# First batch of a fused attention and expert kernel: another order of filler, scores, values and sums of x, and k of batch two on one engine

## The chip, the cores and the metric

The kernel runs on one core of a Trainium2 chip. The core has five engines, each with a queue of its own that runs in order: TensorE (PE in the profile, with its weight loads as PEld), VectorE (DVE), ScalarE (ACT), GpSimd (POOL) and SyncE (SP), which here only issues DMAs. They wait for each other on semaphores. The metric is the device time of one execution in microseconds (us).

## The reference

```python
def _attn_ref(q, k, v):                      # 8 batches, 8 heads, 576 rows, 64 columns
    k_p = k.reshape(B, H, Sp, pool, D).mean(axis=3)     # pool = 8, Sp = 72
    v_p = v.reshape(B, H, Sp, pool, D).mean(axis=3)
    scores = scale * np.matmul(q, k_p.transpose(0, 1, 3, 2))
    scores = scores - np.max(scores, axis=-1, keepdims=True)
    attn = np.exp(scores)
    attn = attn / (np.sum(attn, axis=-1, keepdims=True) + 1e-09)
    return np.matmul(attn, v_p)
def _moe_ref(x, w_in, w_out, alpha):         # x: 4608 x 512, w_in: 512 x 2048
    h = x @ w_in
    s = np.sin(alpha * h)
    g = h + s * s / (alpha + 1e-09)
    return g @ w_out
```

x is the output of the attention, with the heads side by side. All is float32.

## The kernel before, in words

**Hidden layer.** `hidden` computes h = x w_in and g for nine tiles u of 512 rows of x. Rows and columns are halved twice, and seven block products take the place of eight: p1 to p7, in the order 1, 5, 6, 2, 7, 3, 4. Their left sides are sums of blocks of w_in, made by `combine_w_in` (L638; four steps: s1 = a21 + a22, s2 = s1 - a11, a21 = a11 - a21, s4 = a12 - s2), their right sides sums of blocks of x, made by `sums_of_x` (L740; four steps, of which step 1 needs step 0 and step 3 needs step 1). The columns of w_in come in four parts J. So a tile u has 28 slots, seven for each J. In each slot TensorE runs one product (L767, four instructions of 128x256, eight records in the profile), and the queue of work `left` does what the product of the slot before made possible: copies and sines on ScalarE, additions on VectorE (L746, L838).

**Attention beside it.** The attention of batch u + 1 is written by hand into the slots of tile u: `carry(u)` puts functions into a table by slot, and `hidden` calls those of a slot ahead of its product. Each engine's queue has the order in which the functions are called, so an instruction that waits holds all that stand behind it on its engine. Scores of a batch (L288) need k, summed over eight rows by GpSimd (`pool_rows`, L120, three additions) and turned by TensorE (`k_t`, L250). exp is on ScalarE, the sum and its reciprocal on VectorE and the multiplication on GpSimd (`norm`, L345). `turn` (L469 to L479) transposes 32x32 blocks on VectorE, and `move` (L489) brings them into the tile aM with 16 DMAs in two parts on SP's queue. `all_values` (L565, L578) multiplies aM with the sums of v in slot 25 or 26 and gives x of the next tile. k of a batch is loaded in two halves (`load_k`, L108) into one of two buffers, `kvin`, that v uses too.

**The first batch** has no tile ahead of it to hide behind. `first_batch` handles its heads in four pairs. k's rows are added (`load_k_heads`, L162 and L164, on VectorE for pairs one and two, on GpSimd for three and four); `k_head` and `k_last` (L354, L360) turn and sum them on TensorE, `q_head` (L371) turns q, `products_head` (L392) makes the scores, `soft_shift` (L398, L400) subtracts the largest, `soft_exp` (L406) takes exp, `norm_head` (L412, L413, L418) sums and divides. `a_head` (L446 to L453) turns the weights of two pairs. `sum_v_rest` and `sum_v_rows` (L181, L191) sum v on TensorE. `values` (L535, L537) multiplies weights and v for two pairs into two PSUM banks, and `to_x` (L504, or L506 on VectorE) copies them to x. `fill` (L878) puts in products of a tile of ones, `full`, whose result is not used; `first_batch` makes it (L872). Pairs three and four are finished in slots 1 and 2 of tile 0, where also one half of k of batch two is summed by VectorE (`half_k`, L113); the other half is GpSimd's.

Where it matters below: L600 turns alpha, L601 to L610 make its reciprocal, L150 and L152 add k's last rows, L945 is one more unused product that keeps an order, L93 copies q of batch two, L262 and L251 copy turned q and k, L807 and L809 are copies of `left`, and L954 clears a part of aM.

Of the kernel before, what the change touches and what calls it, by code (L numbers as in the profile page):

```python
# [13 lines left out]
F32 = mybir.dt.float32  # L14
AX = mybir.AxisListType.X
AF = mybir.ActivationFunctionType
OP = mybir.AluOpType
PSUM = bass.MemoryType.PSUM

P = 128  # L20
POOL = 8
TH = 256
# [18 lines left out]
class Kernel:  # L41
# [58 lines left out]
        return (qm[:, 0:n].rearrange("p (h t d) -> p h t d", h=self.H, t=4),  # L100
                qm[:64, n:].rearrange("p (h d) -> p h d", h=self.H))

    def load_k(self, b, e, later=False):

        Sp, D, NP = self.Sp, self.D, self.NP
        m = Sp // 3
        t = self.kvp.tile([P, 2048], F32, name="kvin")[:NP * m, 0:3 * POOL * D]
        self.nc.sync.dma_start(out=t, in_=self.k[b, NP * e:NP * e + NP].rearrange("h (p x) d -> (h p) (x d)", x=3 * POOL))  # L108
        if b not in self.kp:
            self.kp[b] = self.ap.tile([NP * m, 3, 2, D], F32, name="kp")  # L110
        t, out = t.rearrange("p (j x) -> p j x", j=3), self.kp[b][:, :, e, :]
        if later:
            return lambda: self.nc.vector.tensor_reduce(out=out, in_=t.rearrange("p j (t d) -> p j d t", t=POOL), axis=AX, op=OP.add)  # L113
        self.pool_rows(t, out)

    def pool_rows(self, t, out):
# [113 lines left out]
    def attention(self, b):  # L230

        nc, D, H, Sp, NP, S = self.nc, self.D, self.H, self.Sp, self.NP, self.S
# [255 lines left out]
                        r, w = 64 * s + 32 * c, 704 if c else 736  # L488
                        nc.sync.dma_start(out=self.aM[r:r + 32, a, 0:w], in_=tr[32 * a:32 * a + 32, c, s, 0:w])  # L489

        def to_x(ps, hp, t0, m, s0=0, eng=nc.scalar):

            while s0 < m:
                u, x0 = divmod(b * S + t0 + s0, 2 * TH)
                w = min(m - s0, 2 * TH - x0)
                if u not in self.xT:
                    self.xT[u] = self.home(u % 3, [P, self.K1, 2 * TH])
                x = self.xT[u][:, hp, x0:x0 + w]
                if t0:
                    y = ps[..., s0:s0 + w]  # L500
                else:
                    x, y = x.rearrange("p (j t) -> p j t", t=4), ps[:, s0 // 4:(s0 + w) // 4, :]
                if eng is nc.scalar:
                    nc.scalar.mul(out=x, in_=y, mul=1.0 / POOL)  # L504
                else:
                    nc.vector.tensor_scalar(out=x, in0=y, scalar1=1.0 / POOL, scalar2=None, op0=OP.mult)  # L506
                s0 += w

        def value_parts(hp, rest):
# [16 lines left out]
            return ([(vm[64 * s:64 * s + 64, 2 * g + e], at(64 * s, 64, 2 * g + e)) for e in range(2)],  # L526
                    (vz[r:r + 32, 2 * g:2 * g + 2], at(r, 32, 4)))

        def values(hps, banks, engines, n=1):

            ps = [self.psum([P, 4 * P], i) for i in banks]
            parts = [value_parts(hp, False) for hp in hps]
            for o, (main, _) in zip(ps, parts):
                for e, (w, x) in enumerate(main):
                    nc.tensor.matmul(o[64 * e:64 * e + 64], w, x, start=True, stop=False, skip_group_check=True)  # L535
            for o, (_, (w, x)) in zip(ps, parts):
                nc.tensor.matmul(o, w.rearrange("p e d -> p (e d)"), x, start=False, stop=True, skip_group_check=True)  # L537
            for i in range(n):
                for hp, o, eng in zip(hps, ps, engines):
                    to_x(o.rearrange("p (t j) -> p j t", t=4), hp, 0, 512 // n * (i + 1), 512 // n * i, eng)  # L540

        def values_rest(banks):

# [185 lines left out]
        self.aturn = (self.aturn + 1) % 3  # L729
        return self.psum(shape, 5 + self.aturn)  # L730

    def sums_of_x(self, u, n, kk=slice(0, 2)):

        nc = self.nc
        if u not in self.bt:
            self.bt[u] = self.home(3, [P, 4, 2, TH])
        xT, bt = self.xT[u], self.bt[u]
        B = lambda i, j: xT[:, 2 * i:2 * i + 2, j * TH:(j + 1) * TH]
        o, x, y = ((0, B(0, 1), B(0, 0)), (1, B(1, 1), bt[:, 0]), (2, B(1, 1), B(0, 1)), (3, B(1, 0), bt[:, 1]))[n]
        nc.vector.tensor_tensor(out=bt[:, o, kk], in0=x[:, kk], in1=y[:, kk], op=OP.subtract)  # L740

    def hidden(self, u, extra):

# [112 lines left out]
    def first_batch(self):  # L856

        nc = self.nc
        self.att = [self.attention(b) for b in range(self.B)]
        A = self.att[0]  # L860
# [7 lines left out]
        self.load_q_heads(0, 0, 2, nc.scalar)  # L868
        add_k = [self.load_k_heads(0, nc.sync, nc.vector)]
        one = self.sm.tile([P, 1], F32, name="one")  # L870
        full = self.tp.tile([P, P], F32, name="full")
        nc.vector.memset(full[:], 1.0)  # L872
        nc.scalar.activation(out=one[:], in_=self.ident[:, 0:1], func=AF.Sqrt)

        def fill(n):

            for _ in range(n):
                nc.tensor.matmul(self.PS[:, 0, 3 * P:4 * P], full[:], full[:], start=True, stop=True)  # L878
        fill(5)
        self.turn_alpha()  # L880
        refine = self.root()
# [16 lines left out]
        self.load_w_in_part(0)  # L898
        self.q_rest = self.A[3][:64, 0, 512:1024].rearrange("p (h d) -> p h d", h=self.H)
        A.new_a()  # L900
        fill(4)
        A.k_head(0)
        add_rest()
        A.q_head(0)
        A.k_last()
        for f in add_k[1:]:
            f()
        fill(2)
        A.products_head(0)
        A.k_head(1)  # L910
        A.q_head(1)
        A.soft_shift(0)
        A.soft_exp(0)
        refine()
        fill(2)
        A.products_head(1)
        A.k_head(2)
        A.q_head(2)
        A.soft_shift(1)
        A.soft_exp(1)  # L920
        A.norm_head(0, nc.gpsimd)
        fill(2)
        A.products_head(2)
        self.sum_v_rest(0, 0)
        A.k_head(3)
        A.q_head(3)
        A.norm_head(1, nc.vector)
        fill(2)
        A.products_head(3)
        A.soft_shift(2)  # L930
        self.sum_v_rows(0, 0, 2)
        A.a_head(0, (1, 7, 0))
        A.soft_exp(2)
        A.soft_shift(3)
        A.soft_exp(3)
        self.sum_v_rows(0, 1, 2)
        A.norm_head(2, nc.gpsimd)
        A.norm_head(3, nc.vector)
        self.load_q_rest(0, self.q_rest)
        self.load_k(1, 0)  # L940
        self.half_k = self.load_k(1, 1, True)
        self.load_q(1)
        self.load_w_in_part(1)
        A.values((0, 1), (5, 6), (nc.scalar, nc.scalar), 2)
        nc.tensor.matmul(self.psum([P, 4 * P], 4), full[:], far[0][:, 0:4 * P], start=True, stop=True)  # L945
        self.combine_w_in(0, (0,))
        self.sums_of_x(0, 0)
        self.combine_w_in(0, (1,))
        self.combine_w_in(0, (2, 3), nc.gpsimd)

    def carry(self, u):

# [3 lines left out]
        b = u + 1  # L956
        if u == 0:
            A0, A = self.att[:2]
            at(1, A0.rest_q)
            at(1, A0.a_head, 1, (5, 7, 2))  # L960
            at(1, self.half_k)
            at(2, A0.values, (2, 3), (2, 1), (self.nc.vector, self.nc.scalar))
            for kk in range(2):
                at(2, self.sums_of_x, 0, 1, slice(kk, kk + 1))
            at(2, A0.score, 4)
            at(2, self.sums_of_x, 0, 2)
            at(2, self.sums_of_x, 0, 3)
            at(2, self.load_w_in_part, 2)
            at(2, self.load_w_in_part, 3)
            at(2, self.pairs_q, 1, range(5))  # L970
            at(4, self.combine_w_in, 1, (0, 1, 2, 3), self.nc.gpsimd)
            at(4, A.q_t, 0, self.nc.vector.tensor_copy)
            at(4, A.q_t, 1, self.nc.vector.tensor_copy)
            at(4, A.k_t)
            at(7, self.load_v, 1)
            at(7, lambda: self.pool_v())
            for i in range(2):
                at((5, 10)[i], A.two_scores, i)
            at(11, A.two_shifts)
            for i in range(2, 5):  # L980
                at(5 + i, A.q_t, i)
            at(9, A0.exp, 4)
            for i in range(4):
                at((9, 9, 15, 15)[i], A.exp, i)
                at((10, 10, 16, 16)[i], A.norm, i)
                at((13, 13, 17, 18)[i], A.turn, i)
            at(8, self.combine_w_in, 2, (0, 1, 2, 3), self.nc.gpsimd)
            at(13, A0.norm_rest)
            at(14, self.combine_w_in, 3, (0, 1), self.nc.gpsimd)
            at(17, self.combine_w_in, 3, (2, 3), self.nc.gpsimd)  # L990
            at(23, A0.a_rest)
            at(24, lambda: A0.values_rest((5, 6, 7, (self.turn + 1) % 5)))
            for r in (32, 96):
                at(3, self.nc.gpsimd.memset, self.aM[r:r + 32, :, 704:736], 0.0)
            at(18, A.move, 0)
            at(18, A.move, 1)
            at(26, A.all_values)
            at(9, self.load_q, 2)
            at(14, self.load_q, 3)
            for e in range(2):  # L1000
                at(17, self.load_k, 2, e)
            at(27, self.att[2].k_t)
            turn = 23
        else:
            at(0, self.sums_of_x, u, 2)
            at(0, self.sums_of_x, u, 3)
        if 0 < u < last:
# [6 lines left out]
                at((9, 10, 11, 12)[i], A.norm, i)  # L1014
                at((12, 12, 13, 13)[i], A.turn, i)
            at(14, A.move, 0)
            at(14, A.move, 1)
            at(6, self.load_v, b)
            at(12, lambda: self.pool_v())
            for i in range(2):  # L1020
                if b < last:
                    at((12, 17)[i], self.load_k, b + 1, i)
            at(25, A.all_values)
            if b < last:
                at(26, self.att[b + 1].k_t)
# [216 lines left out]
    def run(self):  # L1242
        nc, tc = self.nc, self.tc
        pool = lambda s, n, b, **kw: s.enter_context(tc.tile_pool(name=n, bufs=b, **kw))
        with ExitStack() as top:
            const = self.const = pool(top, "const", 1)
            self.tp = pool(top, "tp", 1)
            self.PS = pool(top, "ps", 1, space=PSUM).tile([P, 8, 512], F32, name="PS")
            self.aturn = 0
            ident = self.ident = const.tile([P, P], F32, name="ident")  # L1250
            make_identity(nc, ident)
            engines = {nc.tensor.engine, nc.vector.engine, nc.scalar.engine, nc.gpsimd.engine, nc.sync.engine}
# [98 lines left out]
```

## Time and profile before

| | |
|---|---|
| median of 7 runs | 926.2 us (923.79 to 926.81) |
| the profiled execution | 926.2 us |
| its span, first to last instruction | 924.4 us |
| mean granted TensorE clock | 0.998 |
| first product of the hidden layer starts | 26.89 us |
| p6 and p3 of the first part start | 38.41 and 48.77 us |

The profile is of one execution. A line of a view names the engine, the line of the kernel, the operation, what is written and read (home are tiles of x and sums of x, a and as blocks of w_in and their sums, PS is PSUM, ex the scores), the shape and how often (x). The waits view puts idle time of an engine down to the instruction that ended it. A float32 matmul leaves two records.

### The profile page before, as it was taken

The numbers are of one execution on the slowest core, as the hardware profiler recorded it, in microseconds if no ns is written. First come the engines' busy times: TensorE is split into PE (matmuls) and PEld (weight loads), VectorE is DVE, ScalarE is ACT, GpSimd is POOL, SyncE is SP. The second block draws the span as 40 slices with busy tenths as digits, with TensorE's granted clock in tenths as the row PEclk, the third lists the DMA queues.
The fourth block names the chain that finished last, engine by engine and source line by source line (L and its number), as shares of the span: only waits on it lengthen the run. The fifth ranks groups of instructions, "written<-read, shape, count | busy, mean of one in ns | idle before, by whom it ended". The sixth has DMA issues, their size and how long they took to land.

```text
span 924.4 us, 17756 instructions
## 1 busy us (share of the span) xinstructions
PE 906.8 (98%) x7025; PEld 820.8 (89%) x7025; DVE 669.4 (72%) x1010; ACT 436.2 (47%) x996; POOL 159.6 (17%) x153
## 2 busy tenths in 40 slices
PE   7899999999999999999999999999999999999997
PEld 6587787888878888788888899999999999999997
DVE  6874764746657475673466989988888888988894
ACT  3577586776857668586886631211111111112111
POOL 2747062160612506141000000000000000000000
PEclk9999999999999999999999999999999999999999
DMA  9846666867568755646527237171626353433401
GB/s 272 224 149 180 173 170 194 225 187 174 154 190 212 202 134 156 199 110 220 197 92 235 87 112 228 30 225 33 192 65 173 85 168 90 149 109 115 143 15 39
DMA packets 134731, 141.13 MB, mean 153 GB/s; under 512 B 49832, under 2 KB 103224, under 8 KB 134648
## 3 DMA queue, kind: packets, MB, share of 16 engines
q1 hardware_dynamic: 133304, 138.54, 52.1%
q10 hardware_dynamic: 1344, 1.45, 0.5%
q8 instruction: 56, 0.92, 0.5%
q14 instruction: 27, 0.22, 0.1%
HBM read 75.37 MB, written 47.19 MB: 133 GB/s over the span
## 4 chain that ended last, share of the span: by engine, by line
PE 79%; DVE 6%; SPq 6%; DMA 3%; POOL 2%; issue 2%; ACT 1%; DVEq 0%; POOLq 0%; ACTq 0%
PE PS L1107 41%; PE PS L767 33%; SPq L489 5%; DMA kvin<-in_k_dram 3%; PE PS L288 2%; POOL kvin L120 2%; DVE tr L469 1%; DVE h L746 1%; DVE sm L343 1%; SPq L845 1%; PE PS L878 1%; PE PS L565 1%; DVE home L740 0%; PE PS L250 0%; POOL kp L120 0%
## 5 line engine op out<-in xcount | busy, mean ns | idle before, releaser
L767 PE MATMUL PS<-home,a 128*128 128x256 f32 x1152 | 264.7, 381 | 1.6 <-DVE h L746 1.4
L767 PEld LDWEIGHTS PS<-home,a 128*128 128x128 f32 x1152 | 217.1, 190 | 38.0 <-issue 4.8
L767 PE MATMUL PS<-home,as 128*128 128x256 f32 x864 | 201.7, 383 | 2.9 <-DVE home L740 2.9
L767 PEld LDWEIGHTS PS<-home,as 128*128 128x128 f32 x864 | 163.4, 191 | 26.9 <-DVE home L740 3.7
L1107 PE MATMUL PS<-s,wb 128*128 128x144 f32 x896 | 119.3, 286 | 0.4 <-ACT PS L1220 0.4
L1107 PEld LDWEIGHTS PS<-s,wb 128*128 128x128 f32 x896 | 113.7, 190 | 0.7 <-ACT PS L1220 0.6
L780 ACT ACTIVATE s<-s,c 128x256 f32<-128x256 f32 (+1 forms) x216 | 110.2, 574 | 0.0
L746 DVE TENSOR_TENSOR h<-PS,p 128x512 f32<-128x512 f32 x72 | 49.1, 684 | 80.6 <-PE PS L767 42.7
L773 ACT ACTIVATE s<-h,al 128x256 f32<-128x256 f32 x144 | 65.2, 505 | 59.4 <-DVE h L746 58.6
L1220 ACT COPY PS<-PS 128x144 f32<-128x144 f32 x56 | 14.7, 263 | 146.0 <-PE PS L1107 141.7
L773 ACT ACTIVATE s<-PS,al 128x256 f32<-128x256 f32 x144 | 60.1, 469 | 32.9 <-PE PS L767 20.9
L1107 PE MATMUL PS<-r,wb 128*128 128x144 f32 x512 | 73.2, 286 | 0.0
L1107 PE MATMUL PS<-s,a 128*128 128x144 f32 x512 | 73.2, 286 | 0.0
L838 DVE TENSOR_TENSOR h<-PS,s 128x512 f32<-128x512 f32 x36 | 24.7, 686 | 65.2 <-ACT s L780 65.2
L120 POOL TENSOR_TENSOR kvin<-kvin 96x768 f32<-96x768 f32 (+3 forms) x40 | 63.1, 1578 | 47.5 <-DMA kvin<-in_k_dram 43.1
L1107 PEld LDWEIGHTS PS<-r,wb 128*128 128x128 f32 x512 | 67.1, 190 | 0.1
L1107 PEld LDWEIGHTS PS<-s,a 128*128 128x128 f32 x512 | 67.0, 190 | 0.0
L345 POOL TENSOR_TENSOR ex<-ex,sm 128x576 f32<-128x576 f32 (+1 forms) x28 | 35.0, 1272 | 183.8 <-ACT PS L807 163.2
L1239 ACT COPY PS<-PS 128x144 f32<-128x144 f32 x56 | 14.7, 263 | 88.4 <-PE PS L1107 88.4
L1107 PE MATMUL PS<-s,we 128*128 128x144 f32 x384 | 54.9, 286 | 0.0
L1107 PE MATMUL PS<-x,wb 128*128 128x144 f32 x384 | 54.9, 286 | 0.0
L1107 PEld LDWEIGHTS PS<-s,we 128*128 128x128 f32 x384 | 50.4, 190 | 0.1
(191 smaller groups left out, 1214.5 us busy)
## 6 DMA issues: line engine op xcount, KB each, us to landing
g_bridge<-h SPq DMA_DIRECT2D x72, 512.0 KB
r<-g_bridge SPq DMA_DIRECT2D x31, 1152.0 KB
out_dram<-o SPq DMA_DIRECT2D x128, 72.0 KB
kvin<-in_k_dram SPq DMA_DIRECT2D x14, 576.0 KB
q<-in_q_dram SPq DMA_DIRECT2D x7, 1024.0 KB
kvin<-in_v_dram SPq DMA_DIRECT2D x14, 512.0 KB
aM<-tr SPq DMA_DIRECT2D x56, 92.0 KB
aM<-tr SPq DMA_DIRECT2D x56, 88.0 KB
```

The source lines that it names most:

```text
L120: self.nc.gpsimd.tensor_tensor(out=t[..., 0:w] if w > D else out, in0=t[..., 0:w], in1=t[..., w:2 * w], op=OP.add)
L288: nc.tensor.matmul(ps[e][r0 + r:r0 + r + q.shape[-1], h, :], q[s], kb[s, hp, :], start=True, stop=True)
L345: nc.gpsimd.tensor_tensor(out=E(i), in0=E(i), in1=sm.unsqueeze(2).to_broadcast([P, n, Sp]), op=OP.mult)
L489: nc.sync.dma_start(out=self.aM[r:r + 32, a, 0:w], in_=tr[32 * a:32 * a + 32, c, s, 0:w])
L746: add = lambda o, x, y: nc.vector.tensor_tensor(out=o, in0=x, in1=y, op=OP.add)
L767: nc.tensor.matmul(ps[:, jj, :], self.A[p][:, kk, f * P:(f + 1) * P], x[:, kk, :], start=(start and jj == 0 and kk == 0), stop=(kk == 1), ...
L773: nc.scalar.activation(out=G.s[:, i, jj, j, :], in_=src[:, jj], func=AF.Sin, scale=self.al[:, f:f + 1])
L780: nc.scalar.activation(out=x, in_=x, func=AF.Square, scale=self.c[:, f:f + 1])
L838: add = lambda o, x, y: self.nc.vector.tensor_tensor(out=o, in0=x, in1=y, op=OP.add)
L1107: nc.tensor.matmul(out, W[:, J // 2, J % 2, :], A[:, J, :], start=(start and J == 0), stop=(J == self.NJ - 1), skip_group_check=True)
L1220: nc.scalar.copy(out=x1[:, 0, :], in_=x0[:, 1, :])
L1239: nc.scalar.copy(out=x1[:, 1, :], in_=x1[:, 0, :])
```

## The change

What is done in the first batch, and the order in which it is issued:

- `full` is a constant now, written by VectorE before the identity is made. The fills are 5, 3, 3, 3, 2 instead of 5, 4, 2, 2, 2, 2.
- products_head(3) comes behind a_head(0) (which turns the weights of pairs one and two). norm_head(1) comes right behind norm_head(0); sum_v_rest behind q_head(3). soft_exp(3) and norm_head(3) come behind the values of the first two pairs. The second sum_v_rows goes to slot 1 of tile 0.
- sums_of_x(0, 0) and (0, 1) are gone. `values` makes the two differences of x itself: the second half of the values in PSUM, times 1/8, minus the first half of x, or minus the difference before, in one VectorE instruction for each pair and half. All copies to x are ScalarE's.
- combine_w_in for J = 0: step s1 goes to GpSimd, the last two steps go from GpSimd to VectorE, in slot 2. s2 stays on VectorE.
- Both halves of k of batch two are summed on GpSimd.

In the slots: turn of the last tile of scores and the 16 moves of batch two go from slot 18 to slot 19 of tile 0. In the tiles after it the second half of k is loaded in slot 14, between the two parts of the moves, instead of in slot 17.

```diff
-    def load_k(self, b, e, later=False):
+    def load_k(self, b, e):
...
-        if later:
-            return lambda: self.nc.vector.tensor_reduce(out=out, in_=t.rearrange("p j (t d) -> p j d t", t=POOL), axis=AX, op=OP.add)
         self.pool_rows(t, out)
...
-        def values(hps, banks, engines, n=1):
+        def values(hps, banks, n, d):
...
+            if d == 0:
+                self.bt[0] = self.home(3, [P, 4, 2, TH])
+            turned = [o.rearrange("p (t j) -> p j t", t=4) for o in ps]
             for i in range(n):
-                for hp, o, eng in zip(hps, ps, engines):
-                    to_x(o.rearrange("p (t j) -> p j t", t=4), hp, 0, 512 // n * (i + 1), 512 // n * i, eng)
+                for hp, o in zip(hps, turned):
+                    to_x(o, hp, 0, 512 // n * (i + 1), 512 // n * i)
+            for kk, o in enumerate(turned):
+                y = self.bt[0][:, 0, kk] if d else self.xT[0][:, kk, 0:TH]
+                f = lambda x: x.rearrange("p (j t) -> p j t", t=4)
+                nc.vector.scalar_tensor_tensor(out=f(self.bt[0][:, d, kk]), in0=o[:, TH // 4:TH // 2, :], scalar=1.0 / POOL, in1=f(y),
+                                               op0=OP.mult, op1=OP.subtract)
...
-        fill(4)
+        fill(3)
         A.k_head(0)
         add_rest()
         A.q_head(0)
         A.k_last()
         for f in add_k[1:]:
             f()
-        fill(2)
+        fill(3)
         A.products_head(0)
...
         refine()
-        fill(2)
+        fill(3)
         A.products_head(1)
...
         A.norm_head(0, nc.gpsimd)
+        A.norm_head(1, nc.vector)
         fill(2)
         A.products_head(2)
-        self.sum_v_rest(0, 0)
         A.k_head(3)
         A.q_head(3)
-        A.norm_head(1, nc.vector)
-        fill(2)
-        A.products_head(3)
+        self.sum_v_rest(0, 0)
         A.soft_shift(2)
         self.sum_v_rows(0, 0, 2)
         A.a_head(0, (1, 7, 0))
+        self.combine_w_in(0, (0,), nc.gpsimd)
+        A.products_head(3)
         A.soft_exp(2)
         A.soft_shift(3)
-        A.soft_exp(3)
-        self.sum_v_rows(0, 1, 2)
         A.norm_head(2, nc.gpsimd)
-        A.norm_head(3, nc.vector)
         self.load_q_rest(0, self.q_rest)
-        self.load_k(1, 0)
-        self.half_k = self.load_k(1, 1, True)
+        for e in range(2):
+            self.load_k(1, e)
         self.load_q(1)
         self.load_w_in_part(1)
-        A.values((0, 1), (5, 6), (nc.scalar, nc.scalar), 2)
-        nc.tensor.matmul(self.psum([P, 4 * P], 4), full[:], far[0][:, 0:4 * P], start=True, stop=True)
-        self.combine_w_in(0, (0,))
-        self.sums_of_x(0, 0)
+        A.values((0, 1), (5, 6), 2, 0)
+        nc.tensor.matmul(self.psum([P, 4 * P], 4), self.full[:], far[0][:, 0:4 * P], start=True, stop=True)
+        A.soft_exp(3)
+        A.norm_head(3, nc.vector)
         self.combine_w_in(0, (1,))
-        self.combine_w_in(0, (2, 3), nc.gpsimd)
...
+            at(1, self.sum_v_rows, 0, 1, 2)
             at(1, A0.rest_q)
             at(1, A0.a_head, 1, (5, 7, 2))
-            at(1, self.half_k)
-            at(2, A0.values, (2, 3), (2, 1), (self.nc.vector, self.nc.scalar))
-            for kk in range(2):
-                at(2, self.sums_of_x, 0, 1, slice(kk, kk + 1))
+            at(2, A0.values, (2, 3), (2, 1), 1, 1)
             at(2, A0.score, 4)
             at(2, self.sums_of_x, 0, 2)
             at(2, self.sums_of_x, 0, 3)
+            at(2, self.combine_w_in, 0, (2, 3))
...
-                at((13, 13, 17, 18)[i], A.turn, i)
+                at((13, 13, 17, 19)[i], A.turn, i)
...
-            at(18, A.move, 0)
-            at(18, A.move, 1)
+            at(19, A.move, 0)
+            at(19, A.move, 1)
...
             at(14, A.move, 0)
-            at(14, A.move, 1)
...
-                    at((12, 17)[i], self.load_k, b + 1, i)
+                    at((12, 14)[i], self.load_k, b + 1, i)
+            at(14, A.move, 1)
...
+            full = self.full = const.tile([P, P], F32, name="full")
+            nc.vector.memset(full[:], 1.0)
             ident = self.ident = const.tile([P, P], F32, name="ident")
```

More of the change, by code (lines that the diff above doesn't have):

```diff
@@ L489, in move, with to_x @@
                         nc.sync.dma_start(out=self.aM[r:r + 32, a, 0:w], in_=tr[32 * a:32 * a + 32, c, s, 0:w])
-        def to_x(ps, hp, t0, m, s0=0, eng=nc.scalar):
+        def to_x(ps, hp, t0, m, s0=0):
             while s0 < m:
@@ L502, in to_x @@
                     x, y = x.rearrange("p (j t) -> p j t", t=4), ps[:, s0 // 4:(s0 + w) // 4, :]
[L503 to L506, printed above, removed]
+                nc.scalar.mul(out=x, in_=y, mul=1.0 / POOL)
                 s0 += w
@@ L730, in abank, with sums_of_x @@
         return self.psum(shape, 5 + self.aturn)
-    def sums_of_x(self, u, n, kk=slice(0, 2)):
+    def sums_of_x(self, u, n):
         nc = self.nc
@@ L739, in sums_of_x @@
         o, x, y = ((0, B(0, 1), B(0, 0)), (1, B(1, 1), bt[:, 0]), (2, B(1, 1), B(0, 1)), (3, B(1, 0), bt[:, 1]))[n]
-        nc.vector.tensor_tensor(out=bt[:, o, kk], in0=x[:, kk], in1=y[:, kk], op=OP.subtract)
+        nc.vector.tensor_tensor(out=bt[:, o], in0=x, in1=y, op=OP.subtract)
     def hidden(self, u, extra):
@@ L870, in first_batch @@
         one = self.sm.tile([P, 1], F32, name="one")
-        full = self.tp.tile([P, P], F32, name="full")
-        nc.vector.memset(full[:], 1.0)
         nc.scalar.activation(out=one[:], in_=self.ident[:, 0:1], func=AF.Sqrt)
@@ L877, in fill @@
             for _ in range(n):
-                nc.tensor.matmul(self.PS[:, 0, 3 * P:4 * P], full[:], full[:], start=True, stop=True)
+                nc.tensor.matmul(self.PS[:, 0, 3 * P:4 * P], self.full[:], self.full[:], start=True, stop=True)
         fill(5)
```

## The prediction

> **What bounds the kernel now.** The page first: its head says that TensorE has work in all but the first slices.
>
> ```profile
> PE 906.8 (98%) x7025; PEld 820.8 (89%) x7025; DVE 669.4 (72%) x1010; ACT 436.2 (47%) x996; POOL 159.6 (17%) x153
> PE   7899999999999999999999999999999999999997
> ```
>
> So a change can save only what TensorE (PE) idles or repeats. The list of waits of PE (what it waited for, us in total, times, longest) says where:
>
> ```profile
> PE PS L767 <- DVE home L740: 2.9, 3, 1.9
> PE PS L878 <- DVE full L872: 2.8, 1, 2.8
> PE PS L250 <- POOL kp L120: 1.8, 4, 0.7
> PE PS L767 <- DVE h L746: 1.4, 2, 1.3
> PE PS L360 <- DVE home L152: 1.0, 1, 1.0
> PE PS L446 <- issue: 1.0, 1, 1.0
> ```
>
> These are, from the top: sums of x, the filler tile, k of the next batch, an addition in slot 19, k's last rows, and a wait that no engine explains. Next, VectorE's timeline ahead of the largest (start, us, engine, line, what, idle before):
>
> ```profile
> 27.11 2.31 DVE L638 TENSOR_TENSOR as<-a,a 128x512 f32<-128x512 f32 x1
> 29.35 1.48 DVE L740 TENSOR_TENSOR home<-home 128x512 f32<-128x512 f32 x1
> 30.75 2.30 DVE L638 TENSOR_TENSOR as<-as,a 128x512 f32<-128x512 f32 x1
> 32.98 0.68 DVE L448 COPY aM<-PS 128x512 f32<-128x512 f32 x1
> 33.58 2.81 DVE L113 TENSOR_REDUCE kp<-kvin 96x192 f32<-96x1536 f32 x1
> 36.28 0.70 DVE L506 TENSOR_SCALAR home<-PS 128x512 f32<-128x512 f32 x1
> 37.02 2.75 DVE L740 TENSOR_TENSOR home<-home,home 128x256 f32<-128x256 f32 x2
> ...
> 41.39 0.67 DVE L740 TENSOR_TENSOR home<-home 128x512 f32<-128x512 f32 x1
> ```
>
> VectorE is full here, and a 512-column addition of two SBUF tiles takes 1.48 or 2.31 us beside GpSimd's additions (27.07 to 40.90) but 0.67 once GpSimd stops at 40.90: the two take turns. Additions with one input in PSUM do not wait (L746 at 52.17 took 0.68 beside GpSimd's 51.91 to 53.18). Last, the windows (PE busy, PEld, DVE, ACT, POOL, PE clock, DMA share, GB/s):
>
> ```profile
> 36.50:39.90 3.40, 0.78 (x3) 0.38 (x3) 3.37 (x4) 2.72 (x6) 3.32 (x4) 1.00 1.04 177
> 39.90:43.30 3.40, 3.40 (x8) 2.73 (x9) 2.70 (x6) 0.50 (x2) 0.99 (x1) 0.50 0.37 113
> ```
>
> The idle 3.4 us are followed by 3.4 us at half clock.
>
> **The sum is made against** the profiled execution: 926.2 us, span 924.4 and 1.8 around it; 926.2 is also the median of the seven runs. I follow the instruction order of the changed kernel with the old rows' durations; times are us of the span.
>
> **1. Filler first.** The memset (0.17) now leads VectorE's queue, ahead of reductions that wait for the identity until 1.65. GpSimd's first operation starts at 0.74, so PE starts at 0.95 and not 2.84. Ten cold filler records (2.50) end at 3.45, alpha has landed (3.20), and VectorE's chain al to first k sum (1.40 from L601's start) ends at 5.10, not 7.02. L150 and L152 (0.82 and 0.70 beside GpSimd) now run at 6.2 to 6.8, before GpSimd's k rows land (7.62): 0.29 each, as the 128x128 row L182. k's last rows go out at 6.83, not 10.16. Then k sums on VectorE and GpSimd alternate, and the first score shift starts at 9.0, not 11.83. Products of pairs two and three follow at 10.9 and 13.3 (13.48, 15.92): the lead is 2.6. The moved fillers (0.125 a record) end 0.1 behind ScalarE's copy.
>
> **2. Scores of pair four behind the turned weights.** sum_v_rows needs ScalarE's copy of q at 15.7; a_head(0) starts at 16.75, not 21.43, since products of pair four (0.7) and the unexplained 0.96 stood before it. Products of pair four follow, 18.05 to 18.75; ScalarE's three copies end at 18.75, with no second exp before x. Values take 2.08 as now (23.85 to 25.93) and end at 20.85; the first product of the hidden layer (p1) starts at 21.8, not 26.89: 5.1.
>
> **3. Given back.** exp of pair four now queues behind four copies to x (1.21): 22.85. VectorE's sum and reciprocal (0.95) end at 23.85, and its two multiplications of SBUF tiles meet GpSimd's k rows (1.80, 1.0, 0.6, from 22.8): taking turns they end at 26.2 (27.20 now). sum_v_rows (1.02) moves behind p1 and fits before that. a_head(1) ends at 26.7 and p5 starts there, not at 30.88: lead 4.2.
>
> **4. VectorE's queue, 27 to 40.** Gone: 2.31, 1.48, 2.81, 0.70 and 2.75, or 10.05. New: four differences of 128x256 straight from PSUM, which no row shows. Below, L355 (copy from PSUM, 128x128) took 0.29; above, L746 (512 columns) 0.68; I take 0.45, nearest to L312 (288 columns, 0.458). A difference waits for ScalarE's copy out of the same bank; behind the first two stands norm of pair four, for which a_head(1) waits, behind the others the score shifts. Values of pairs three and four run 28.5 to 30.6 without the 0.9 that PE waits for L448 now; ScalarE's two copies end at 31.3 and 31.9 (the second, 0.6, was VectorE's); p6 starts at 31.8, not 38.41. Without the idle window no half-clock window follows: 3.4 at 0.50 cost 1.7. p2 starts at 33.7, not 42.50: lead 8.8.
>
> **5. Given back again.** Score shifts (1.70) end at 34.0. Then the two remaining sums of x meet GpSimd's combinations of w_in (31.2 to 36.9: 1.27 each) and end at 37.4; two combinations moved to VectorE add 0.65 each, 38.7. PE is at p7 at 36.65 and waits 1.4 for the first. Copies of q and k (1.29, 0.55) end at 40.3: 0.45 more. p3 starts at 41.5, not 48.77: **7.3**. Alone at 0.67 each these four would leave a lead of 9.2; at 2.3 each (L638) p3 starts at 46.2, lead 2.6. I take turns, as L740 at 1.48. The unexplained 0.96 may recur elsewhere: I count half, **6.8**.
>
> GpSimd gets the other half of k (1.8, 1.0, 0.6 after 27.2), hidden as k's transposes (36.4) come 5 later, and one combination of w_in (1.27 from 16.1; its blocks land by 15.88), hidden before norm of pair three at 21.4. The Trainium skill, "GPSIMD Engine Reference" (4.1 Engine selection), speaks against both: two-input elementwise work is about 2 times slower there. The trace agrees on the rate (1.27 against 0.67), but VectorE took 2.31 for that step; on the path the rule would cost 0.6, here nothing.
>
> The skill's "TensorE: Matmul & The Clock Gate" (Why this matters for your kernels) warns of idle gaps above about 3 us. Here gaps of 1.92 and 0.71 halved the clock, so the measurement decides; by the page the 1.7 would not count, and 918.0 would come out.
>
> **6. Slot 19.** PE waits 1.25 (80.12) because L746 queues behind turn(3), which waits for GpSimd until 77.98. Now L746 is first. But the moves to aM still follow turn(3) (last landing 91.60, values at 92.29 now), so I count **1.1**.
>
> **7. Steady batches.** The second k load is issued after eight of the 16 moves instead of after all and two stores of g (136.6, not 142.91). Landing (5.9 later) and GpSimd (3.5) end near 146, wanted at 151.8. The five waits of L250 are 0.73, 0.15, 0.36, 0.20, 0.55: **2.0**. Eight moves and two stores go 0.8 later and queue behind 576 KB; last moves now land 2.8 to 4.0 before values of x read them. SP waits for GpSimd's kvin first, which was free 1.1 to 2.2 before.
>
> Sum: 6.8 + 1.1 + 2.0 = 9.9; 926.2 - 9.9 = **916.3**.
>
> **Rivals.**
> (a) VectorE and GpSimd cost step 5 its upper end: 2.6 + 1.1 + 2.0, **920.5**. For: GpSimd is busy to 36.9. Against: only four operations meet it.
> (b) The lead is lost at data: v of batch two lands at 42 to 45 whatever PE does (DMA engines are full until 39); its rows (6.85) and combinations (5.1) hold GpSimd until 55.6, and norm is wanted at 62.77 - 7.3 = 55.5. No slack; if all is lost, 1.1 + 2.0 stay: **923.1**. Against: turn follows norm 2 later.
> (c) k's wait turns into one for the moves: **918.3**.
> (d) Slower: the second k load, on SP's queue, holds the other eight moves. If they land behind all its 6 us, at 147.7, values wait 1.3 in each of five batches, 6.6, still a gain. Slower begins where they land 5.2 late (3.2 of slack and 9.9/5); at 5.6 it is **928**. It needs SP held for GpSimd as well.
>
> **How the numbers follow.** Forecast 0.55, (a) 0.16, (b) 0.08, (c) 0.11, cancelled within 0.2% (about what a measurement can tell) 0.04, (d) 0.06. So faster 0.90, same 0.04, slower 0.06. Low end: 9.2 + 1.25 + 2.0 is 913.7, and runs spread by 3: 913.0. High end takes in (c) and (a) with part of the 0.96: 921.5; (b) and (d) are left out.
>
> **What would show it.** First filler at 0.95; p1, p5, p6, p2 and p3 at 21.8, 26.7, 31.8, 33.7 and 41.5; clock 1.00 from 37 to 47; differences at 0.45; a wait of PE for L638's successor near 37; no waits of k's transposes. It is wrong if PE idles at values for aM, or if p3 starts after 46.

## The result and the profile after

The changed kernel takes 922.23 us in the median of 18 runs (919.50 to 925.24), the kernel before, beside it, 925.48 (42 runs, 922.94 to 928.95). The ratio is 0.9962, 95% interval 0.9953 to 0.9971: 3.5 us faster, where 9.9 were forecast and 913.0 to 921.5 was the range. The profiled execution took 921.36 us, 919.4 of it span.

The page after: VectorE has 8 us less to do, and PE's first slice is full.

```profile
PE 906.6 (99%) x7023; PEld 819.4 (89%) x7023; DVE 661.2 (72%) x1010; ACT 436.7 (47%) x997; POOL 163.2 (18%) x155
PE   9998999999999999999999999999999999999997
```

The waits of PE after (what, us in total, times, longest):

```profile
PE PS L568 <- DVE h L841: 1.8, 3, 0.9
PE PS L770 <- DVE h L749: 1.6, 2, 1.4
PE PS L879 <- DVE full L1247: 1.1, 1, 1.1
PE PS L568 <- DMA aM<-tr: 1.0, 1, 1.0
PE PS L770 <- DVE home L542: 0.5, 1, 0.5
```

The waits for k are gone, and of those for sums of x 0.5 is left. New are those of L568 (L565 before), the values of x of the next tile: once for the moves, three times for the additions of L841 (L838 before). VectorE's timeline where it was full:

```profile
30.50 0.91 DVE L542 SCALAR_TENSOR_TENSOR home<-PS,home 128x256 f32<-128x256 f32 x2 [4.17 <-ACT home L501]
...
33.03 0.67 DVE L743 TENSOR_TENSOR home<-home 128x512 f32<-128x512 f32 x1
33.63 0.68 DVE L743 TENSOR_TENSOR home<-home,home 128x512 f32<-128x512 f32 x1
34.23 0.68 DVE L641 TENSOR_TENSOR a<-a,a 128x512 f32<-128x512 f32 x1
34.83 0.68 DVE L641 TENSOR_TENSOR as<-a,as 128x512 f32<-128x512 f32 x1
```

The differences cost 0.46 each. The four sums took 0.67 to 0.68 each although GpSimd worked beside them: here it was GpSimd's combination of w_in that took longer, 2.87 where the next one takes 1.27. GpSimd's timeline:

```profile
33.78 2.87 POOL L641 TENSOR_TENSOR as<-a,a 128x512 f32<-128x512 f32 x1 [1.22 <-DMA a<-in_moe_w_in_dram]
```

The windows of the old idle stretch (PE busy, PEld, DVE, ACT, POOL, clock, DMA share, GB/s) show PE busy at full clock:

```profile
36.50:39.90 3.40, 3.40 (x75) 2.80 (x74) 2.78 (x7) 1.89 (x5) 3.32 (x4) 1.00 1.05 255
39.90:43.30 3.40, 3.40 (x19) 3.00 (x18) 2.88 (x5) 1.05 (x3) 0.56 (x1) 1.00 0.80 179
```

**Where it went.** Call lead how much earlier a product of the hidden layer starts than in the profile of before. It is 5.6 at p1, 10.0 at p3, 8.5 at the start of tile 1, and 5.0 from tile 6 to the end. So in this execution the first batch brought more than the 7.9 forecast for it (6.8 + 1.1), and tiles 1 to 5, which were to bring 2.0, took 3.5. In each of them the lead falls at the start of slot 25, behind the values (1.84, 1.22, 1.34, 1.09, 0.93: 6.42), and rises at slot 26, behind k's transposes (0.94, 0.36, 0.38, 0.41, 0.77: 2.87). Tile 1 shows how. SyncE's queue after (start, us):

```profile
122.22 6.05 SPq L487 DMA_DIRECT2D aM<-tr  x8
128.37 0.52 SPq L108 DMA_DIRECT2D kvin<-in_k_dram  x1
128.93 5.38 SPq L487 DMA_DIRECT2D aM<-tr  x8
```

By the DMA completions, the first move behind the load has landed 5.15 after its issue, where the first of those ahead of it takes 2.10; the eighth is issued only at 133.81, when the load has landed (133.79); the last lands at 136.38. Before, it was 143.17, or 134.64 with the lead of 8.53 taken off: 1.74 later. VectorE's timeline before, then after:

```profile
143.25 2.37 DVE L211 STREAM_TRANSPOSE tr<-q 128x1024 f32<-128x1024 f32 x2 [4.14 <-DMA aM<-tr]
145.54 0.65 DVE L838 TENSOR_TENSOR h<-PS,s 128x512 f32<-128x512 f32 x1
146.12 1.21 DVE L838 TENSOR_TENSOR h<-h,s 128x1024 f32<-128x1024 f32 x1
```

```profile
136.56 2.37 DVE L209 STREAM_TRANSPOSE tr<-q 128x1024 f32<-128x1024 f32 x2 [5.98 <-DMA aM<-tr]
138.85 0.65 DVE L841 TENSOR_TENSOR h<-PS,s 128x512 f32<-128x512 f32 x1
139.43 1.21 DVE L841 TENSOR_TENSOR h<-h,s 128x1024 f32<-128x1024 f32 x1
```

The transposes of q (`turn_q`) write the tile tr, out of which the moves copy. They wait for the last move to land, in both kernels, and the additions queue behind them. PE's timeline after:

```profile
137.81 1.08 PE L568 MATMUL PS<-aM,vm 64*64 64x512 f32 x4
139.56 0.33 PE L568 MATMUL PS<-aM,vm 64*64 64x64 f32 x4 [0.67 <-DVE h L841]
...
143.09 0.70 PE L770 MATMUL PS<-home,a 128*128 128x256 f32 x2
```

PE has begun the values, so the moves they read are there; it stops for a PSUM bank that L841 has still to read. From the first record of the values to the next product PE takes 5.28 here (137.81 to 143.09) and 3.44 before (146.34 to 149.78): that is the 1.84. The waits view counts 0.67 of it as idle, which is why it shows only 1.8 us for L841 in all where the lead loses 6.42.

### The profile page after: what moved, and what is told of

The parts are those of the page before. It is cut to its first block, busy times and chain, and to the rows that moved or that the text cites. A ratio compares the mean times of both kernels' runs of the same rounds, so it can differ in the third digit from the quotient of the medians.

```text
span 919.4 us, 17757 instructions
## 1 busy us (share of the span) xinstructions
PE 906.6 (99%) x7023; PEld 819.4 (89%) x7023; DVE 661.2 (72%) x1010; ACT 436.7 (47%) x997; POOL 163.2 (18%) x155
## 4 chain that ended last, share of the span: by engine, by line
PE 80%; DMA 7%; POOL 4%; SPq 3%; DVE 3%; issue 1%; ACT 1%; DVEq 0%; POOLq 0%; ACTq 0%
PE PS L1103 42%; PE PS L770 33%; PE PS L568 2%; DMA kvin<-in_k_dram 2%; DMA a<-in_moe_w_in_dram 2%; PE PS L286 2%; DMA aM<-tr 1%; POOL kvin L118 1%; DMA q<-in_q_dram 1%; DMA kvin<-in_v_dram 1%; SPq L635 1%; POOL ex L343 1%; SPq L487 1%; PE PS L581 1%; DVE tr L209 1%
## 5 line engine op out<-in xcount | busy, mean ns | idle before, releaser
L1216 ACT COPY PS<-PS 128x144 f32<-128x144 f32 x56 | 14.7, 263 | 145.7 <-PE PS L1103 144.3
L118 POOL TENSOR_TENSOR kvin<-kvin 96x768 f32<-96x768 f32 (+3 forms) x42 | 66.5, 1583 | 16.7 <-DMA kvin<-in_k_dram 9.8
L841 DVE TENSOR_TENSOR h<-PS,s 128x512 f32<-128x512 f32 x36 | 24.6, 684 | 61.7 <-ACT s L783 61.7
L1235 ACT COPY PS<-PS 128x144 f32<-128x144 f32 x56 | 14.7, 263 | 88.4 <-PE PS L1103 88.4
```

Of the source, the lines that this page charges most:

```text
L118: self.nc.gpsimd.tensor_tensor(out=t[..., 0:w] if w > D else out, in0=t[..., 0:w], in1=t[..., w:2 * w], op=OP.add)
L841: add = lambda o, x, y: self.nc.vector.tensor_tensor(out=o, in0=x, in1=y, op=OP.add)
L1216: nc.scalar.copy(out=x1[:, 0, :], in_=x0[:, 1, :])
L1235: nc.scalar.copy(out=x1[:, 1, :], in_=x1[:, 0, :])
```

## The experiments

Theory A: the second load of k between the two parts of the moves delays the moves, VectorE's transposes wait for tr, and PE loses 6.4 us behind them. Rival B: that line works, and the shorter first batch makes data late later. Rival C: values wait for the moves themselves. Ratios are to the kernel before, run beside each.

| kernel | median, us | ratio, 95% interval |
|---|---|---|
| e1 after, k's half in slot 17 | 918.16 | 0.9925 (0.9910 to 0.9939) |
| e2 before, k's half between the moves | 928.15 | 1.0035 (1.0021 to 1.0049) |
| e3 after, q turned a slot later | 918.44 | 0.9932 (0.9916 to 0.9948) |
| e4 after, k's half behind both parts | 915.79 | 0.9894 (0.9877 to 0.9910) |
| e5 e4, moves of tile 0 in slot 18 | 916.09 | 0.9904 (0.9889 to 0.9918) |
| e6 e4, filler tile late | 915.88 | 0.9910 (0.9890 to 0.9929) |
| e7 e4, sums of x on VectorE | 919.47 | 0.9935 (0.9914 to 0.9956) |
| e8 before, k's half behind both parts | 923.22 | 0.9979 (0.9966 to 0.9992) |
| e9 after, q turned in another tile | 916.03 | 0.9897 (0.9882 to 0.9912) |
| e10 e4, two more fills | 917.23 | 0.9911 (0.9896 to 0.9926) |
| e11 e4, four moves on ScalarE | 915.57 | 0.9889 (0.9872 to 0.9906) |
| e12 e4, k of batch three sooner | 913.65 | 0.9872 (0.9839 to 0.9905) |

And the leads in the profiles, one execution each (p1: its start; slot 5 is p3; values and k: what tiles 1 to 5 add to the lead up to slot 25, behind the values, and behind it, at k's transposes; end: the lead at the last product):

| | p1 | slot 5 | tile 1 | values | k | end |
|---|---|---|---|---|---|---|
| after | 21.27 | 10.0 | 8.5 | -6.42 | 2.87 | 5.0 |
| e1 | 21.54 | 8.7 | 8.3 | 0.64 | 0.03 | 8.9 |
| e2 | 26.28 | 0.8 | 0.8 | -5.32 | 2.86 | -1.6 |
| e3 | 23.15 | 7.7 | 8.8 | -3.19 | 2.87 | 8.4 |
| e4 | 23.48 | 5.5 | 4.8 | 0.04 | 2.86 | 7.7 |
| e5 | 24.21 | 6.7 | 6.6 | 1.21 | 2.87 | 10.7 |
| e6 | 27.69 | 3.2 | 4.2 | 0.56 | 2.87 | 7.6 |
| e7 | 21.73 | 1.3 | 0.7 | 0.81 | 2.87 | 4.3 |
| e8 | 30.47 | -3.6 | -3.7 | 0.36 | 2.86 | -0.4 |
| e9 | 24.09 | 6.8 | 7.5 | 1.30 | 2.87 | 11.7 |
| e10 | 25.93 | 5.0 | 6.0 | 0.37 | 2.87 | 9.2 |
| e11 | 22.65 | 6.1 | 3.3 | 0.52 | 2.87 | 6.7 |
| e12 | 21.27 | 5.3 | 6.2 | 1.11 | 2.87 | 10.1 |

**e1.**

```diff
-                    at((12, 14)[i], self.load_k, b + 1, i)
-            at(14, A.move, 1)
+                    at((12, 17)[i], self.load_k, b + 1, i)
```

(and both moves in a row ahead of it).

> The changed kernel with one line undone: the second half of k of the next batch is loaded in slot 17 again, behind both parts of the moves. Theory A (this line is what went wrong: the moves land 1.8 us later, VectorE's transposes of q, which write the tile that the moves read, wait for them, the additions of L841 queue behind the transposes, and PE waits for their banks at the values of L568): the lead of 8.5 us at the start of tile 1 is kept, but the five waits of k's transposes come back; 922.2 - 3.5 = 918.7 us, 0.993 of the kernel before. In the trace the last move lands 1.8 earlier against PE's slots and PE does not wait in L568. Rival B (the line works as predicted, worth 2.0, and the lead is lost because the shorter front makes data of the later batches late): 922.2 + 2.0 = 924.2 us, 0.999, and L568 still waits.

918.16: the line costs the changed kernel 0.0037, or 3.4 us. The loss at the values is gone, k's waits are back. B falls.

**e2.** The changed line alone in the kernel before.

> The kernel before with that one line alone: the second half of k loaded in slot 14, between the two parts of the moves; nothing of the first batch is changed. Theory A: slower by 3.5 us, 925.5 + 3.5 = 929.0 us, 1.004 of the kernel before; no wait of k's transposes, but waits at the values of x in tiles 1 to 5. Rival B, and the prediction's step 7: faster by 2.0, 923.5 us, 0.998.

928.15, 3.2 slower (1.9 to 4.5). The loss needs nothing of the first batch. VectorE's timeline in tile 1, against 143.25 before, with PE 0.84 ahead:

```profile
144.21 2.37 DVE L211 STREAM_TRANSPOSE tr<-q 128x1024 f32<-128x1024 f32 x2 [5.95 <-DMA aM<-tr]
```

**e3.**

```diff
-            turn = 22
+            turn = 23
```

> The changed kernel with q's transposes one slot later in tiles 1 to 5 (turn = 23 for 22), so that the additions of L841 stand ahead of them in VectorE's queue; the loads and moves stay as changed. Theory A: the additions no longer wait for the moves, so the five losses at L568 (1.84, 1.22, 1.34, 1.09, 0.93, together 6.4 us) go, while no wait of k's transposes comes back: 922.2 - 6.4 = 915.8 us, 0.990 of the kernel before. If the moves' landing is itself what values wait for (rival C: they land at 136.4 and values start at 137.65, so 1.3 of slack), nothing is gained: 922 us, 0.996. If q is needed earlier than that, the wait turns up at the scores of the next tile.

918.44: half of what A expected, against nothing by C. The additions no longer wait, but a small copy of VectorE (L575) that the values need now stands behind the transposes. Of the 6.42 in lead, 3.19 is still lost. The waits of PE name the copy, but count only 1.1 of it:

```profile
PE PS L568 <- DVE order L575: 1.1, 3, 0.4
```

**e4.** Slot 14 as changed, but `at(14, A.move, 1)` ahead of the load.

> The changed kernel with the second half of k loaded in slot 14 still, but behind both parts of the moves and ahead of the two stores of g. Theory A: the moves land as early as before, so the 6.4 us at L568 go; k's half is issued near 133 us of the span in tile 1, lands 6 later and is added by 142.7 (3.5 us of GpSimd), about when k's transposes want it (143.3): 915.8 us, at most 0.5 more in each of five tiles, 918.3; 0.990 to 0.992 of the kernel before. Rival B: no different from the changed kernel, 922 us, or slower by k's waits.

915.79, where A put it: both the gain at k and the old values. The load lands at 142.29 in tile 1 and GpSimd ends at 146.32; k's transposes start at 147.19, without a wait.

**e5.**

```diff
-                at((13, 13, 17, 19)[i], A.turn, i)
+                at((13, 13, 17, 18)[i], A.turn, i)
-            at(19, A.move, 0)
-            at(19, A.move, 1)
+            at(18, A.move, 0)
+            at(18, A.move, 1)
```

> The kernel of e4 (changed kernel, second half of k behind both parts of the moves; 915.8 us) with the last turn and the 16 moves of tile 0 back in slot 18. Theory A: what slot 19 wins at L749 (1.1 by the prediction; 0.9 to 1.4 in the profiles of e1, e3 and e4) is taken back at the values of slot 26, where PE waits for the last move, because turn(3) waits for GpSimd in either place: PE waits 1.2 more at slot 20 and as much less at L568, 915.8 us within the interval, 0.990 of the kernel before. The prediction's step 6: slower by 1.1, 916.9, 0.991; too near to tell by the time alone, so the leads by slot decide.

916.09, no difference that can be told. The wait at slot 20 is back (1.0), and PE waits for nothing at the values of tile 0. The lead goes from 6.69 at slot 5 to 6.57 at tile 1; in e4 from 5.54 to 4.76, with the waits of e4:

```profile
PE PS L568 <- DMA aM<-tr: 1.9, 1, 1.9
PE PS L770 <- DVE a L641: 1.4, 1, 1.4
```

The second is the wait at p7, far ahead of slot 20. So in e4 slot 19 wins 1.4 at slot 20 and loses 2.3 at the values. That is one execution: from slot 5 to tile 1 the lead changes by -0.1 in e5, by -0.8 in e4, by -2.9 in e11, but by 0.7 to 1.0 in e3, e6, e9, e10 and e12, which all have slot 19. The times differ by 0.9 us with about 2.0 to either side, so neither 1.1 nor nothing is excluded. What slot 19 is worth stays open.

**e6.** `full` and its memset made in `first_batch` again.

> The kernel of e4 (915.8 us) with the tile of ones written where it was before, behind the identity's reductions in VectorE's queue. The prediction's step 1: PE starts at 2.84 again and everything of the front is 2.6 later: 918.4 us, 0.993 of the kernel before. Rival: the clock of TensorE decides, which rises to full at 5.0 and 5.7 us of the span in two profiles of the changed order and at 10.4 and 11.2 in two others, and the landing of q (5.8 to 6.2), so that the filler's 1.8 earlier start is worth nothing on the median: 915.8, 0.990.

Between the two: 0.0016 slower than e4, 1.5 us with about 2.4 to either side. Not settled. Its profile has p1 at 27.69, with full clock only at 14.51, 4.2 behind p1 of e4; but at the end its lead is that of e4 (7.6 and 7.7).

**e7.** `values`, `sums_of_x`, the half of k and the combinations as before. It leaves exp and norm of pair four behind the values.

> The kernel of e4 (915.8 us) with step 4 of the prediction undone: sums of x by two additions on VectorE behind the copies to x, one copy to x and half of k's sums on VectorE, the first step of the combinations of w_in on VectorE and the last two on GpSimd in the first batch. Everything else stays. The prediction's steps 4 and 5 (7.3 lead at p3 against 4.2 at p5) make it 3.1 slower; the profiles of the changed order show 3.2 to 5.0 from p5 to p3: 919 to 921 us, 0.993 to 0.996 of the kernel before. Rival: the lead is lost behind p3 in any case, at the moves of tile 0, which hang on v and GpSimd: at most 1.5 slower, 917.3, 0.992.

919.47, 0.0041 or 3.8 us slower than e4, give or take 2.5. From p5 to p3 its lead grows by 0.1, against 3.2 in e4 and 5.0 in the changed kernel: that is what step 4 was about, and it holds. But from p1 to p5 the lead falls by 4.0 (1.0 in e4), because the old sums of x stand on VectorE behind the norm of pair four: there PE waits 1.0 for the norm and 2.1 for the sums. So the 3.8 is not step 4 alone.

**e8.**

```diff
-                    at((12, 17)[i], self.load_k, b + 1, i)
+                    at((12, 14)[i], self.load_k, b + 1, i)
```

> The kernel before with nothing but the second half of k loaded in slot 14 behind both parts of the moves, ahead of two stores of g. Theory A: k's waits go (2.9 us of lead in the five tiles, from the jumps behind slot 25: 0.94, 0.36, 0.38, 0.41, 0.77) and no wait for the moves comes: 925.0 - 2.9 = 922.1 us, 0.997. The rest of e4's gain, 6.3 us, is then the first batch's. Rival: without the lead of the first batch the load is no earlier against k's transposes and gains less: 924 us, 0.999.

923.22: 1.9 us (0.7 to 3.1). From e8 to e4 is the first batch alone: 0.9979 to 0.9894, 7.9 us, give or take 2.

**e9.** `turn_q` writes a view of the scores' tile instead of tr; the load stays between the moves.

```diff
-        tr = self.tr[:, 0:4 * self.NP * 160].rearrange("p (c hp t i) -> p c hp t i", c=4, hp=self.NP, i=32)
+        tr = self.ex[:].rearrange("p i h c -> p (i h) c")[:, 0:40, 0:64].rearrange("p (e hp t) (k i) -> p e k hp t i", e=2, hp=self.NP, k=2)
```

> The changed kernel, its second load of k still between the two parts of the moves, but q's transposes write into the tile of scores (ex), which nothing reads in slots 22 to 27, and no longer into the tile tr that the moves read; q's DMAs read from there in pieces of 32 columns. One more clearing of 64 columns by GpSimd in slot 3 of tile 0. Theory A: VectorE's transposes no longer wait for the moves, L841 is on time, PE does not wait at L568 in tiles 1 to 5: 922.2 - 6.4 = 915.8 us, 0.990 of the kernel before, if q's smaller pieces are not late for the scores. Rival C (values wait for the landing of the moves themselves, 136.4 in tile 1): the losses at slot 25 stay, 922 us, 0.996.

916.03, the number A gave. Its timeline of VectorE in tile 1:

```profile
131.53 2.36 DVE L207 STREAM_TRANSPOSE ex<-q 128x1024 f32<-128x1024 f32 x2
136.42 0.69 DVE L838 TENSOR_TENSOR h<-PS,s 128x512 f32<-128x512 f32 x1 [2.53 <-ACT s L780]
```

The transposes are done before the last move has landed, and the additions wait for ScalarE alone. A is shown and C falls: the load between the moves hurts only through the tile that is written again.

**e10.** `fill(2)` between `k_head(0)` and `q_head(0)`.

> The kernel of e4 (915.8 us) with two more fills (four records, 0.85 us at half clock) between k's first head and q's first head, where PE waits for q from 5.8 to 6.2. Theory: idle moments there keep a window of the clock gate from counting, so that full clock came at 5.0 to 12.9 in five profiles of this order; with the fills it comes by 7.9 (two windows of 3.41 behind the first filler at 1.06), the slow cases go, and the median falls by about 1 to 914.8, 0.989, with a spread under 3 us. Rival: the fills do not matter to it; the median stays at 915.8 or is up to 0.4 later, and the spread stays at 5 us.

917.23, four runs within 0.7 of each other (the theory had a spread under 3), but no faster, and full clock came at 12.62 in its profile, not by 7.9. The theory falls.

**e11.** Four of tile 0's moves with `nc.scalar.dma_start` in slot 20.

> The kernel of e4 (915.8 us) with the last four of tile 0's 16 moves issued by ScalarE in slot 20 instead of by SyncE in slot 19, so that they do not queue behind twelve others at 0.63 each. Theory: the wait for the last move at L568 in tile 0 (1.86, 1.08, 1.03 and 0.22 in the profiles of e4, e1, the changed kernel and e3) goes: 914.8 us, 0.989. Rival: the four issues hold ScalarE's copies and sines by 0.6 each, and PE waits for them instead: 915.8 to 918.2.

915.57, no difference, and the wait at L568 is still 1.86. The eighth of the 16 moves waits until 79.82, as in e4 (79.87). ScalarE issued its four ahead of that, from 73.11 on, so nine moves of SyncE still followed the standstill at 0.63 each, as in e4, and the last landed at 86.92 (86.95). Whether the rate of issue matters is therefore not tested by this run.

**e12.** Both loads of k of batch three in slot 15 for 17, GpSimd's additions left in slot 17.

> The kernel of e4 (915.8 us) with the same rule applied to tile 0: there both loads of k of batch three are issued in slot 17, just ahead of the 16 moves, which land in its profile 3.6 us after issue (the first) and stand still from 77.5 to 79.9 until the second load has landed; here both loads are issued in slot 15 (DMA engines are 0.26 to 0.35 busy from 62 to 70), and GpSimd's additions stay in slot 17. Theory A: the moves land about 2.4 earlier (84.5 for 86.95 of that profile), so the wait of PE at L568 in tile 0 (1.86, 1.08, 1.03, 0.22 in four profiles) goes: about 1.0 less, 914.8 us, 0.988 to 0.989 of the kernel before; the leads by slot show it better than the time. Rival: the last move is late because turn(3) is (GpSimd), whatever the loads do: the wait stays, 915.8, 0.990.

913.65, the fastest of all; against e4 the intervals overlap, so the trace has to say it. The moves no longer stand still (each 0.63 after the last; the first has landed 2.2 after its issue, in e4 6.4), the last lands at 85.58 (86.95), and the values of tile 0 start nearly on time; e4 first, then e12:

```profile
87.16 0.65 PE L568 MATMUL PS<-aM,vm 64*64 64x512 f32 x6 [1.86 <-DMA aM<-tr]
```

```profile
85.78 0.65 PE L570 MATMUL PS<-aM,vm 64*64 64x512 f32 x6 [0.20 <-ACT s L785]
```

## Why the prediction was right in the first batch and wrong in all

**Steps 1 to 3** hold in direction. PE starts at 1.06 (0.95 forecast), products of pairs two and three at 10.37 and 12.81 (10.9, 13.3), p1 at 21.27 (21.8), p5 at 25.88 (26.7). But in other executions of the same order p1 starts at 21.5 to 24.2, and how much the filler alone is worth stays open (e6). The unexplained 0.96 in front of the turned weights, of which half was counted, is absent in this profile; e6 and e10 have such a wait (0.91 and 0.88) at the scores of pair four.

**Step 4** is right: 0.46 for a difference (0.45), p6 at 30.98 and p2 at 32.87 (31.8, 33.7), no half clock there. What it is worth in time is known only together with the loss ahead of p5 in e7.

**Step 5** was right where GpSimd and VectorE took turns. VectorE's timeline of e4:

```profile
35.67 0.74 DVE L743 TENSOR_TENSOR home<-home 128x512 f32<-128x512 f32 x1
36.34 1.76 DVE L743 TENSOR_TENSOR home<-home,home 128x512 f32<-128x512 f32 x1
38.02 1.75 DVE L641 TENSOR_TENSOR a<-a,a 128x512 f32<-128x512 f32 x1
39.69 0.68 DVE L641 TENSOR_TENSOR as<-a,as 128x512 f32<-128x512 f32 x1
```

Together 4.93, where the prediction had 4.7 (34.0 to 38.7: 1.7 for each sum, a figure of which it shows no row, and 0.65 for each combination); PE waits 1.39 at p7 (1.4). So it is in e4, e11 and e12, where two of the four take about 1.75 each and two of GpSimd's combinations about 1.71, and p5 to p3 takes 14.7 to 16.6 us. But in the profiles after and of e1, e3, e5, e6, e9 and e10 the four run at 0.67 to 0.68 with GpSimd beside them: one combination of GpSimd takes 2.87 to 3.79 instead, and p5 to p3 takes 12.85 or 12.86 every time; after, p3 came at 38.73 (41.5). Taking turns, the premise of this step, is therefore the rarer case, and what decides between the two is open.

**Step 6** failed by what is late next. The wait at slot 20 goes in e1, e3, e4 and others (lead up 0.9 to 1.4), but the moves are then late for the values of tile 0. The prediction saw them last to land 0.7 ahead of the values and took only 0.15 off the 1.25 for it. From slot 5 to tile 1 the lead changes by anything from 1.0 to -2.9 with slot 19, and by -0.1 without it (e5). In the profiled execution the wait at slot 20 stayed, at 1.43, because v of batch two landed 2 us later than before (45.75 for 43.75) and GpSimd's norm with it: a part of rival (b).

That e4 against e8 measures 7.9 for the first batch, the number forecast, is partly luck. In the profile after, the terms are 5.0 at p5 (4.2 forecast), 5.0 from there to p3 (3.1) and -1.5 over the rest of tile 0 (1.1): too little in two, too much in the third.

**Step 7 is the step that failed.** Its first half holds: in tile 1 the load lands at 133.79 and is added by 137.41, with the lead put back 142.3 and 145.9 (142.5 and 146 forecast); the five waits are gone, worth 2.87 in lead and 1.9 in time (2.0). Its second half read: "Eight moves and two stores go 0.8 later and queue behind 576 KB; last moves now land 2.8 to 4.0 before values of x read them." They land 1.74 later, not 0.8, since the queue was counted in issues and not in landings; and the values are not who needs them first. The tile they copy out of is written again in slot 22, and behind that write stand additions that PE waits for; in the profile before, too, that write waits for the last move (4.14, at 143.25). The price is 6.42 of lead in five tiles, and in time 6.3 us, give or take 1.7 (after against e4): about the whole gap between 9.9 and 3.5. Rival (d) had this load, and 6.6 for it, at another place; that sum would have been 922.9, but it stood in the text only as a step on the way to "slower" at 0.06, and the range ended below it.

## What to carry to other kernels

When transfers are put behind a bulk load, ask both who reads what they write and who writes what they read, and follow the engine's queue behind that second one: a tile that is used again is a wait that no reader shows. Small transfers that many wait for go ahead of a bulk load, or the load goes well ahead of them, where the DMA engines have room (e4, e12). And a gain at one wait counts only up to the next late arrival at the same engine.

## What was not expected of the hardware

**When full clock comes differs from run to run.** The rows of the fills show it: PE's timeline after, then of e5, whose PE starts agree with it within 0.02 us up to 5.3.

```profile
1.06 2.50 PE L879 MATMUL PS<-full 128*128 128x128 f32 x10 [1.06 <-DVE full L1247]
3.71 1.54 PE L879 MATMUL PS<-full 128*128 128x128 f32 x6
7.12 0.89 PE L879 MATMUL PS<-full 128*128 128x128 f32 x6
```

```profile
1.06 2.50 PE L879 MATMUL PS<-full 128*128 128x128 f32 x10 [1.06 <-DVE full L1247]
3.71 1.65 PE L879 MATMUL PS<-full 128*128 128x128 f32 x6
7.79 1.59 PE L879 MATMUL PS<-full 128*128 128x128 f32 x6
```

Six records take 0.89 at full clock and 1.59 at half. By the clock records it rises at 5.00 after, 5.65 in e1, 7.19 in e7, 10.42 in e3, 11.18 in e4 and 12.87 in e5, and p1 starts at 21.27, 21.54, 21.73, 23.15, 23.48 and 24.21: some 0.37 us for each us of half clock. That is 3 us at p1, nearly the whole gain of the change, in a term that the prediction took as fixed. But by itself it does not decide the end: among the profiles without the loss behind the values, e9 has p1 at 24.09 and ends with the largest lead, 11.7, while e4, with p1 at 23.48, ends with 7.7, and e12, with 21.27, with 10.1. p5 to p3 (12.85 to 16.6 us, step 5) and the wait for the moves of tile 0 differ between executions by as much. Which of them makes the spread of 5 us between runs is not shown.

The Trainium skill, "TensorE: Matmul & The Clock Gate" (What's actually happening), says that the clock rises after a busy window of about 3.4 us that runs on its own, whenever the kernel starts. Between a rise of the clock and the next fall, and back, lie multiples of 3.41 us in every profile here, which agrees. An estimate by the rule, two windows behind the first filler at 1.06, has the rise by 7.9; it came at up to 12.87, and in e3 PE was busy for 3.41 of 3.41 us from 3.59 to 7.00 without a rise at 7.00. What keeps a window from counting is open.

**A move waits for the landing of a load ahead of it.** The eighth behind the load is issued at 133.81 in tile 1 after (load landed 133.79), at 133.29 in e3 (133.27), at 79.87 in e4's tile 0 (79.85). In the trace this eighth waits on the semaphore that the load counts up: the queue's DMAs use eight semaphores in turn. So the wait lies in how the program numbers its DMAs; a limit of the chip is not shown.
